# Top-32 attention followed by a SoLU block on one Trainium2 core: the selection of each pair of heads moved one loop step later

## The chip, the cores and the metric

The kernel runs on one core of a Trainium2 chip. The metric is the device time of one execution in microseconds. Before the change it is 2123.96 us, the median of 3 runs (2123.67 to 2125.25). Engines are named as the profile names them: PE (TensorE matmul), PEld (its weight loads), DVE (VectorE), ACT (ScalarE), POOL (GpSimd) and SP (the queue that issues the loads).

## The reference

Attention keeps, in every row of scores, the entries that are not below the 32nd largest; the output goes through a SoLU block.

```python
q, k, v: (8, 8, 576, 64) float32            # batch, heads, seq, head_dim
scores = matmul(q, k.T) / 8
kth    = 32nd largest of each row of scores
scores = where(scores >= kth, scores, -1e9)
attn   = softmax(scores); out = matmul(attn, v)

x  = out as (4608, 512)                      # tokens x (heads * head_dim)
h  = x @ w_in                                # (4608, 1024)
s  = h * softmax(h)
ln = (s - mean(s)) / sqrt(var(s) + 1e-6) * g_ln
y  = ln @ w_out                              # (4608, 512)
```

The weights arrive as 64-bit floats and are converted on the core in the first part of the run.

## The kernel before

Two heads of a batch form a pair; there are 32 pairs (`NPAIR`). A pair has 2 x 576 rows of scores, held as nine row tiles of 128 x 576 (`NT` = 9), in three groups of three (`NG` = 3). The work of a pair i, in functions of the listing:

- `load_qk`, `load_v`: loads of q and k (six transfers) and of v (two), issued on SP.
- `prep`: PE transposes q and k into `qkT`; a few small matmuls give each row a first threshold `t0`, by way of a product `yq`, a DVE sum `ss` and a square root on POOL (`zs`).
- `scores`: PE multiplies into `s_ps`, ACT copies to X (L722), and DVE counts the entries above `t0` (`junkv`, L727). `second` (L735 to L742) makes a better threshold from the counts.
- `count1`: ACT counts against it with a Sign pass that adds up its results (`junka`, L750). `third` (L759 to L767) makes the last threshold `t2`.
- `count2`: ACT's Sign pass against `t2` leaves the signs `sg` (L788) and their sum. Then, in the same function, DVE forms `al` (L793), subtracts it from X and multiplies by the signs (`w`, L799), and takes the eight largest (MAX8, L803): the entries nearest to the threshold, on the side where the 32nd lies.
- `exps`: ACT writes E = exp(X), one instruction for each group (L810). `kth` (from `far`, L816, to L831) picks the 32nd largest from counts and nearest entries.
- `softmax`: DVE masks E by X >= kth and sums it (L841); POOL inverts the sums (`rden`) and scales E (L853).
- `transpose_p`, `transpose_last`, `attn_v`: PE transposes E (`tp_p`, `tp_pt`), ACT copies to PT, and PE multiplies with v (`om`, `ot`); ACT copies the result into `xTm` and `xTt`.

When the four pairs of a batch are done, `queue_batch` appends its token tiles (128 rows of x) to the list `todo`: four tiles, and a fifth with every second batch. A tile has three entries: `mm1` (PE, h_ps, L931), `solu_ln` (DVE, ACT and POOL: hmax, e_sb, solu) and `mm2` (PE `tp_ln` and `o_ps`, L978, then a store). `pop` runs the next entry of the list, if there is one. At first the list holds 18 steps that load and convert the weights.

`slot(i)` joins two pairs: it runs the scores and counts of pair i and the softmax and attention of pair i-1. It is called for i = 0 to 32. Before the change its order is: loads of q and k for pair i+1 and of v for pair i; all scores of i; then for each group `softmax(i-1)`, `count1(i)` alternating with the transposes and attention of i-1, and a pop; then `third(i)`; for each group `count2(i)`, a pop and `exps(i)`; then `prep(i+1)` and `kth(i)`. That is six pops in a full slot.

Nobody writes the engines' queues by hand. The planner of the tile framework walks the program, puts each instruction in its engine's queue when its operands and a buffer for its output are there by the planner's own account, and prefers instructions that stand earlier in the program. On the chip each queue then runs in its order. Buffers are given by tag from a pool: `p1`, `p2`, `p3` and `p6` have 1, 2, 3 and 6 buffers for each tag. X has six (two pairs), E three (one pair), `sg` three (one group), `w` two, q and k two each, `yq` one, s_ps and h_ps share two, in PSUM.

Of the kernel before, what the change touches and what calls it, by code (L numbers as in the profile page):

```python
# [15 lines left out]
P = 128  # L16
# [427 lines left out]
def fast_path(  # L444
# [42 lines left out]
    p2 = ctx.enter_context(tc.tile_pool(name="p2", bufs=2))  # L487
    p3 = ctx.enter_context(tc.tile_pool(name="p3", bufs=3))
    p6 = ctx.enter_context(tc.tile_pool(name="p6", bufs=6))
    small = ctx.enter_context(tc.tile_pool(name="small", bufs=3))  # L490
    ps_big = ctx.enter_context(tc.tile_pool(name="ps_big", bufs=2, space=PS))
    ps_tp = ctx.enter_context(tc.tile_pool(name="ps_tp", bufs=2, space=PS))
# [88 lines left out]
    def load_qk(i):  # L581
        b, hp = pairs[i]
        hh = slice(2 * hp, 2 * hp + 2)
        d = st[i]

        d["q"] = p2.tile([P, NT, D], F32, tag="qm", name="qm")
        d["k"] = p2.tile([P, 2 * NM, D], F32, tag="km", name="km")
        for nm, src in (("q", q), ("k", k)):
            nc.sync.dma_start(
                out=d[nm][:, 0 : 2 * NM, :].rearrange("p (t h) d -> p t h d", h=2),  # L590
                in_=src[b, hh, 0:SM, :].rearrange("h (p t) d -> p t h d", t=NM),
            )
            d[nm + "t"] = p2.tile([ST, 2, D], F32, tag=nm + "t", name=nm + "t")
            nc.sync.dma_start(out=d[nm + "t"], in_=src[b, hh, SM:S, :].rearrange("h p d -> p h d"))
        for h in range(2):
            nc.sync.dma_start(
                out=d["q"][h * ST : (h + 1) * ST, 2 * NM, :], in_=q[b, 2 * hp + h, SM:S, :]
            )
# [10 lines left out]
    def prep(i):  # L609
# [53 lines left out]
                    lhsT=trunc(qkT[hd, 0, qs]), rhs=trunc(mom[hd, :]), start=True, stop=True,  # L663
                )
        ys = [(slice(h, 2 * NM, 2), ys[h]) for h in range(2)] + [(slice(2 * NM, NT), ys[2])]
        yq = p1.tile([P, NT, D], F32, tag="yq", name="yq")
        for js, y in ys:
            nc.vector.tensor_tensor(
                out=yq[:, js, :], in0=y[:, :, 0:D], in1=d["q"][:, js, :], op=ALU.mult
# [25 lines left out]
    def x_of(i, j):  # L695
        return st[i]["X"][j // 3][:, j % 3, :]

    def scores(i, t):

        d = st[i]  # L700
        qkT = d["qkT"]
        tail = t == NM
        if t == 0:
            d["X"] = [None] * NG
            d["c0"] = small.tile([P, NT], F32, tag="c0", name="c0")
        qs = slice(SM, S) if tail else slice(t * P, (t + 1) * P)
        js = [2 * t] if tail else [2 * t, 2 * t + 1]
        big = [ps_big.tile([P, 2, 512], F32, tag="big", name="s_ps") for _ in js]

        for half in range(2):  # L710
            for h in range(2):
                hd = slice(h * D, (h + 1) * D)
                s = big[0][h * ST : (h + 1) * ST] if tail else big[h]
                nc.tensor.matmul(  # L714
                    out=s[:, half, 0:SH], lhsT=qkT[hd, 0, qs],
                    rhs=qkT[hd, 1, half * SH : (half + 1) * SH], start=True, stop=True,
                )
        for j, s in zip(js, big):
            if j % 3 == 0:
                d["X"][j // 3] = p6.tile([P, 3, S], F32, tag="X", name="X")  # L720
            x = x_of(i, j)
            nc.scalar.activation(  # L722
                out=x.rearrange("p (a s) -> p a s", a=2), in_=s[:, :, 0:SH],
                func=AF.Copy, scale=scale,
            )
            junk = p1.tile([P, S], BF16, tag="junkv", name="junkv")
            nc.vector.tensor_scalar(  # L727
                out=junk, in0=x, scalar1=d["t0"][:, j : j + 1], scalar2=None,
                op0=ALU.is_ge, op1=ALU.add, accum_out=d["c0"][:, j : j + 1],
            )  # L730

    def second(i):
        d = st[i]
        r = small.tile([P, NT], F32, tag="r", name="r")
        nc.vector.tensor_scalar(  # L735
            out=r, in0=d["c0"], scalar1=31.5, scalar2=None, op0=ALU.add
        )
        nc.vector.reciprocal(r, r)
        u = small.tile([P, NT], F32, tag="u", name="u")
        nc.vector.tensor_tensor(out=u, in0=r, in1=d["tb"], op=ALU.mult)  # L740
        t1 = small.tile([P, NT], F32, tag="t1", name="t1")
        nc.vector.tensor_tensor(out=t1, in0=u, in1=d["ta"], op=ALU.add)  # L742
        d["u"], d["t1"] = u, t1
        d["n1"] = small.tile([P, NT], F32, tag="n1", name="n1")
        d["n2"] = small.tile([P, NT], F32, tag="n2", name="n2")
# [30 lines left out]
            out=d["tt"], in0=t2, scalar1=2.0, scalar2=1.0, op0=ALU.mult, op1=ALU.mult  # L776
        )

    def count2(i, g):

        d = st[i]
        sg = {}
        for j in range(3 * g, 3 * g + 3):
            sg[j] = p3.tile([P, S], BF16, tag="sg", name="sg")
            nc.scalar.activation(  # L788
                out=sg[j], in_=x_of(i, j), func=AF.Sign, scale=-(1.0 + 2.0**-23),
                bias=d["t2"][:, j : j + 1], accum_out=d["n2"][:, j : j + 1],  # L790
            )
        js = slice(3 * g, 3 * g + 3)
        nc.vector.scalar_tensor_tensor(  # L793
            out=d["al"][:, js], in0=d["n2"][:, js], scalar=512.5, in1=d["tt"][:, js],
            op0=ALU.is_lt, op1=ALU.mult,
        )
        for j in range(3 * g, 3 * g + 3):
            w = p2.tile([P, S], F32, tag="w", name="w")
            nc.vector.scalar_tensor_tensor(  # L799
                out=w, in0=x_of(i, j), scalar=d["al"][:, j : j + 1], in1=sg[j],  # L800
                op0=ALU.subtract, op1=ALU.mult,
            )
            nc.vector.max(d["w8"][:, j, :], w)  # L803
# [206 lines left out]
    def pop():  # L1010
        if todo:
            todo.pop(0)()
# [3 lines left out]
    def slot(i):  # L1016
        new, old = i < NPAIR, i > 0
        if new:
            if i + 1 < NPAIR:
                load_qk(i + 1)  # L1020
            load_v(i)
            for t in range(NM + 1):
                scores(i, t)
            second(i)
        for g in range(NG):
            if old:
                softmax(i - 1, g)
            for j in range(3 * g, 3 * g + 3):
                if new:
                    count1(i, j)  # L1030
                if old:
                    transpose_p(i - 1, j)
                    if j == 3 or j == 7:
                        transpose_last(i - 1, j // 4)
                        attn_v(i - 1, j // 4)
            pop()
        if old:
            transpose_last(i - 1, 2)
            attn_v(i - 1, 2)
        if new:  # L1040
            third(i)
            for g in range(NG):
                count2(i, g)
                pop()
                exps(i, g)
            if i + 1 < NPAIR:
                prep(i + 1)
            kth(i)

    load_qk(0)  # L1050
    prep(0)
# [9 lines left out]


    ok = small.tile([P, 4], F32, tag="ok", name="ok")
    hit = p1.tile([P, NPAIR, NT], F32, tag="yq", name="hit")
    for n, (a, lim, op) in enumerate(
        ((zk_all, 1e-12, ALU.is_gt), (den_all, 1.0, ALU.is_ge), (den_all, 1e30, ALU.is_le))
    ):
# [54 lines left out]
```

## Time and profile before

| | |
|---|---|
| median of 3 runs | 2123.96 us |
| profiled execution, its own time | 2126.24 us |
| its span, first to last instruction | 2124.4 us |
| PE busy | 1522.5 us, 7043 matmuls |
| PEld busy | 847.2 us |
| DVE busy | 1172.9 us, 2816 instructions |
| ACT busy | 1184.7 us, 2398 instructions |
| POOL busy | 649.9 us, 806 instructions |
| mean granted PE clock | 0.795 of full |

The span runs from the first to the last instruction on the core. Busy time is the time in which an engine has an instruction in work. Waits are given as the idle time of the engine just before an instruction, with the instruction whose end let it go on. Line numbers (L799) are those of the listing above. PEclk is the granted TensorE clock as a part of 2.4 GHz; its lower level is 0.5.

### The profile page before, as it was taken

To read this page: it belongs to the slowest core of one execution; us is meant where nothing else is said; L and a number is where in the kernel's file an instruction comes from. 1 tells how busy PE (TensorE), PEld (TensorE's weight loads), DVE (VectorE), ACT (ScalarE), POOL (GpSimd) and SP (SyncE) were. 2 spreads that over 40 slices of the span, in tenths; PEclk is the share of its full clock that TensorE was granted. 3 is DMA by queue.
4 is the path that set the end of the run, shared out by engine and by line. 5 is a ranking of instruction groups with operands and counts; after the bars stand their busy time and mean duration, and the time that the engine had idled before them with its cause. 6 is when DMAs were issued, how large, how long until landed. Compare 5 with 4: busy or idle time off the path is not lost.

```text
span 2124.4 us, 21998 instructions
## 1 busy us (share of the span) xinstructions
PE 1522.5 (72%) x7043; PEld 847.2 (40%) x7043; DVE 1172.9 (55%) x2816; ACT 1184.7 (56%) x2398; POOL 649.9 (31%) x806
## 2 busy tenths in 40 slices
PE   5075558786779777788487785878677877678596
PEld 3043334353334443345243453435333444334343
DVE  4875564565654456555645556456565535655611
ACT  4345555465566455676554565647555755457532
POOL 6776233322312323212233302332232132331221
PEclk8556678976889768896789867988688976889698
DMA  3211000100000100011001010010000100000000
GB/s 103 64 47 38 18 6 17 28 23 18 23 11 18 28 18 23 11 29 28 6 17 28 23 24 6 18 28 23 18 23 11 28 17 18 23 16 11 0 10 17
DMA packets 101900, 48.71 MB, mean 23 GB/s; under 512 B 86920, under 2 KB 95120, under 8 KB 101776
## 3 DMA queue, kind: packets, MB, share of 16 engines
q1 hardware_dynamic: 96528, 37.77, 6.9%
q10 hardware_dynamic: 5248, 9.44, 1.4%
q8 instruction: 59, 0.97, 0.2%
q14 instruction: 65, 0.53, 0.1%
HBM read 37.75 MB, written 9.44 MB: 22 GB/s over the span
## 4 chain that ended last, share of the span: by engine, by line
PE 32%; DVE 27%; ACT 21%; POOL 15%; issue 4%; ACTq 0%; SPq 0%; DMA 0%; DVEq 0%; POOLq 0%
PE o_ps L978 9%; ACT junka L750 8%; DVE w L799 7%; DVE junkv L727 7%; PE om L910 7%; PE s_ps L714 6%; DVE w L803 5%; POOL E L853 4%; ACT sg L788 4%; PE h_ps L931 3%; PE tp_p L870 3%; ACT PT L877 3%; PE tp_ln L972 2%; POOL rden L850 2%; ACT E L810 2%
## 5 line engine op out<-in xcount | busy, mean ns | idle before, releaser
L714 PE MATMUL s_ps<-qkT 64*128 64x288 f32 (+1 forms) x1280 | 367.3, 580 | 34.3 <-ACT X L722 25.6
L870 PE MATMUL tp_p<-ident,E 128*128 128x128 f32 x1152 | 200.7, 315 | 204.9 <-POOL E L853 183.9
L722 ACT ACTIVATE X<-s_ps 128x576 f32<-128x576 f32 x288 | 178.9, 649 | 197.2 <-PE s_ps L714 197.1
L978 PE MATMUL o_ps<-w_out,lnT 128*128 128x512 f32 x576 | 282.8, 648 | 0.0
L750 ACT ACTIVATE junka<-X,t 128x576 bf16<-128x576 f32 x288 | 224.0, 778 | 91.0 <-DVE t L742 88.1
L714 PEld LDWEIGHTS s_ps<-qkT 64*128 64x128 f32 (+1 forms) x1280 | 207.1, 239 | 156.1 <-ACT X L722 98.8
L870 PEld LDWEIGHTS tp_p<-ident,E 128*128 128x128 f32 x1152 | 147.1, 159 | 302.1 <-POOL E L853 212.1
L788 ACT ACTIVATE sg<-X,t 128x576 bf16<-128x576 f32 x288 | 221.9, 773 | 73.3 <-DVE w L799 48.1
L877 ACT COPY PT<-tp_p 128x512 f32<-128x512 f32 x256 | 144.4, 583 | 207.0 <-PE tp_p L870 207.0
L841 DVE SCALAR_TENSOR_TENSOR E<-X,kth,E 128x576 f32<-128x576 f32 x288 | 252.3, 918 | 0.8
L853 POOL TENSOR_SCALAR E<-E,rden 128x576 f32<-128x576 f32 x288 | 247.9, 877 | 9.7
L727 DVE TENSOR_SCALAR_CACHE_REDUCE junkv<-X,t 128x576 bf16<-128x576 f32 x288 | 233.3, 810 | 22.5 <-ACT X L722 6.2
L931 PE MATMUL h_ps<-w_in,xTm 128*128 128x512 f32 x512 | 242.6, 607 | 1.8 <-ACT xTm L916 1.5
L799 DVE SCALAR_TENSOR_TENSOR w<-X,al,sg 128x576 f32<-128x576 f32 x288 | 233.6, 838 | 2.0
L910 PE MATMUL om<-PT,vm 128*64 128x256 f32 x1024 | 188.6, 474 | 62.6 <-ACT PT L877 62.1
L803 DVE MAX8 w<-w 128x8 f32<-128x576 f32 x288 | 208.3, 751 | 1.2
L972 PE MATMUL tp_ln<-ident,solu 128*128 128x128 f32 x288 | 56.7, 351 | 198.4 <-POOL solu L962 197.4
L978 PEld LDWEIGHTS o_ps<-w_out,lnT 128*128 128x128 f32 x576 | 117.8, 210 | 143.1 <-issue 137.9
L810 ACT ACTIVATE E<-X 128x1728 f32<-128x1728 f32 x96 | 157.5, 1640 | 3.6 <-ACT PTt L885 3.3
L775 POOL TENSOR_SCALAR tt<-t 128x9 f32<-128x9 f32 x32 | 6.6, 207 | 479.0 <-DVE t L767 478.8
L957 POOL TENSOR_SCALAR var<-var 128x1 f32<-128x1 f32 x36 | 10.7, 298 | 460.5 <-ACT e_sb L956 460.5
L910 PEld LDWEIGHTS om<-PT,vm 128*64 128x64 f32 x1024 | 94.9, 168 | 135.1 <-ACT PT L877 79.5
(119 smaller groups left out, 1760.9 us busy)
## 6 DMA issues: line engine op xcount, KB each, us to landing
qm<-in_q_dram SPq DMA_DIRECT2D x32, 256.0 KB, 3.4
km<-in_k_dram SPq DMA_DIRECT2D x32, 256.0 KB, 3.4
vm<-in_v_dram SPq DMA_DIRECT2D x32, 256.0 KB, 3.1
out_dram<-osb ACTq DMA_DIRECT2D x32, 256.0 KB, 2.6
w_raw<-in_moe_w_in_dram SPq DMA_DIRECT2D x8, 512.0 KB, 4.0
w_raw<-in_moe_w_out_dram SPq DMA_DIRECT2D x8, 512.0 KB, 3.4
qt<-in_q_dram SPq DMA_DIRECT2D x32, 32.0 KB, 2.3
kt<-in_k_dram SPq DMA_DIRECT2D x32, 32.0 KB, 3.0
```

The costliest lines, as they stand in the source:

```text
L714: nc.tensor.matmul(out=s[:, half, 0:SH], lhsT=qkT[hd, 0, qs], rhs=qkT[hd, 1, half * SH : (half + 1) * SH], start=True, stop=True,)
L727: nc.vector.tensor_scalar(out=junk, in0=x, scalar1=d["t0"][:, j : j + 1], scalar2=None, op0=ALU.is_ge, op1=ALU.add, accum_out=d["c0"][:, j ...
L750: nc.scalar.activation(out=junk, in_=x_of(i, j), func=AF.Sign, scale=-1.0, bias=d["t1"][:, j : j + 1], accum_out=d["n1"][:, j : j + 1],)
L788: nc.scalar.activation(out=sg[j], in_=x_of(i, j), func=AF.Sign, scale=-(1.0 + 2.0**-23), bias=d["t2"][:, j : j + 1], accum_out=d["n2"][:, ...
L799: nc.vector.scalar_tensor_tensor(out=w, in0=x_of(i, j), scalar=d["al"][:, j : j + 1], in1=sg[j], op0=ALU.subtract, op1=ALU.mult,)
L803: nc.vector.max(d["w8"][:, j, :], w)
L841: nc.vector.scalar_tensor_tensor(out=e, in0=x_of(i, j), scalar=d["kth"][:, j : j + 1], in1=e, op0=ALU.is_ge, op1=ALU.mult, accum_out=den_a ...
L853: nc.gpsimd.tensor_scalar(out=e, in0=e, scalar1=d["rden"][:, j : j + 1], scalar2=1.0, op0=ALU.mult, op1=ALU.mult,)
L870: nc.tensor.transpose(tp[:, c, :], pt[:, c * P : (c + 1) * P], ident)
L910: nc.tensor.matmul(out=o[h * D : (h + 1) * D, :], lhsT=vm[:, h, c, :] if c < NM else vt[:, h, :], rhs=rhs[0:ks, c, :], start=(c == 0), sto ...
L931: nc.tensor.matmul(out=h[:, half, :], lhsT=x[:, c, :], rhs=w_in[:, c, half * 512 : (half + 1) * 512], start=(c == 0), stop=(c == NP - 1),)
L978: nc.tensor.matmul(out=o, lhsT=lnT[:, c, :], rhs=w_out[:, c, :], start=(c == 0), stop=(c == NF - 1),)
```

## The change

The functions keep their instructions; their order in `slot` changes, and `count2` is split. `count2(i, j)` is now only the Sign pass of one row tile, whose signs stay in one of nine buffers (`p9`). `nearest(i, g)` holds the DVE part and runs a slot later, with `exps`. The new order of a slot: scores of i, then the loads; then for each group `count1(i)`, `nearest(i-1)`, `exps(i-1)` (in the last group also `third(i)`) and a pop; then `kth(i-1)` and `prep(i+1)`; then for each group `softmax(i-1)`, `count2(i)`, a pop from the second group on, and the transposes and attention of i-1. That is five pops in a full slot. q, k and their tails go from two buffers to one; `yq` and the small tile `hit` at the end share the buffers of `w`.

```diff
+    p9 = ctx.enter_context(tc.tile_pool(name="p9", bufs=9))
...
-        d["q"] = p2.tile([P, NT, D], F32, tag="qm", name="qm")
-        d["k"] = p2.tile([P, 2 * NM, D], F32, tag="km", name="km")
+        d["q"] = p1.tile([P, NT, D], F32, tag="qm", name="qm")
+        d["k"] = p1.tile([P, 2 * NM, D], F32, tag="km", name="km")
...
-            d[nm + "t"] = p2.tile([ST, 2, D], F32, tag=nm + "t", name=nm + "t")
+            d[nm + "t"] = p1.tile([ST, 2, D], F32, tag=nm + "t", name=nm + "t")
...
-        yq = p1.tile([P, NT, D], F32, tag="yq", name="yq")
+        yq = p2.tile([P, NT, D], F32, tag="w", name="yq")
...
-    def count2(i, g):
-        d = st[i]
-        sg = {}
-        for j in range(3 * g, 3 * g + 3):
-            sg[j] = p3.tile([P, S], BF16, tag="sg", name="sg")
-            nc.scalar.activation(
-                out=sg[j], in_=x_of(i, j), func=AF.Sign, scale=-(1.0 + 2.0**-23),
-                bias=d["t2"][:, j : j + 1], accum_out=d["n2"][:, j : j + 1],
-            )
+    def count2(i, j):
+        d = st[i]
+        d["sg", j] = p9.tile([P, S], BF16, tag="sg", name="sg")
+        nc.scalar.activation(
+            out=d["sg", j], in_=x_of(i, j), func=AF.Sign, scale=-(1.0 + 2.0**-23),
+            bias=d["t2"][:, j : j + 1], accum_out=d["n2"][:, j : j + 1],
+        )
+
+    def nearest(i, g):
+        d = st[i]
         js = slice(3 * g, 3 * g + 3)
...
-                out=w, in0=x_of(i, j), scalar=d["al"][:, j : j + 1], in1=sg[j],
+                out=w, in0=x_of(i, j), scalar=d["al"][:, j : j + 1], in1=d.pop(("sg", j)),
...
     def slot(i):
         new, old = i < NPAIR, i > 0
         if new:
+            for t in range(NM + 1):
+                scores(i, t)
             if i + 1 < NPAIR:
                 load_qk(i + 1)
             load_v(i)
-            for t in range(NM + 1):
-                scores(i, t)
             second(i)
+        for g in range(NG):
+            if new:
+                for j in range(3 * g, 3 * g + 3):
+                    count1(i, j)
+            if old:
+                nearest(i - 1, g)
+                exps(i - 1, g)
+            if new and g == NG - 1:
+                third(i)
+            pop()
+        if old:
+            kth(i - 1)
+        if i + 1 < NPAIR:
+            prep(i + 1)
         for g in range(NG):
             if old:
                 softmax(i - 1, g)
             for j in range(3 * g, 3 * g + 3):
                 if new:
-                    count1(i, j)
-                if old:
+                    count2(i, j)
+            if g > 0:
+                pop()
+            if old:
+                for j in range(3 * g, 3 * g + 3):
                     transpose_p(i - 1, j)
                     if j == 3 or j == 7:
                         transpose_last(i - 1, j // 4)
                         attn_v(i - 1, j // 4)
-            pop()
         if old:
             transpose_last(i - 1, 2)
             attn_v(i - 1, 2)
-        if new:
-            third(i)
-            for g in range(NG):
-                count2(i, g)
-                pop()
-                exps(i, g)
-            if i + 1 < NPAIR:
-                prep(i + 1)
-            kth(i)
...
-    hit = p1.tile([P, NPAIR, NT], F32, tag="yq", name="hit")
+    hit = p2.tile([P, NPAIR, NT], F32, tag="w", name="hit")
```

## Rows read from the trace of the kernel before

**Rows 1.** The page, busy us by engine (share of the span) xinstructions.
```profile
PE 1522.5 (72%) x7043; PEld 847.2 (40%) x7043; DVE 1172.9 (55%) x2816; ACT 1184.7 (56%) x2398; POOL 649.9 (31%) x806
```

**Rows 2.** Busy time by stretch (us, each engine's busy us): start, one period, end.
```profile
0.00:452.63 452.63, 269.26 (x1315) 155.92 (x1315) 269.30 (x619) 239.28 (x490) 210.45 (x220) 0.73 0.14 39
...
956.31:1458.06 501.75, 377.29 (x1763) 209.23 (x1762) 282.24 (x687) 295.47 (x599) 134.78 (x179) 0.81 0.08 20
...
1959.82:2124.40 164.58, 119.05 (x451) 62.27 (x450) 56.78 (x140) 58.58 (x111) 35.09 (x49) 0.82 0.03 9
```

**Rows 3.** Busy time by stretch: PE, PEld, DVE, ACT, POOL, then PEclk; slots of a period.
```profile
1010.58:1057.11 46.53, 22.62 (x119) 12.12 (x117) 27.32 (x74) 26.20 (x55) 12.65 (x16) 0.78 0.02 7
1057.11:1122.42 65.31, 55.26 (x235) 29.87 (x237) 36.35 (x89) 37.29 (x76) 18.52 (x25) 0.87 0.06 14
...
1192.21:1270.91 78.70, 59.30 (x284) 35.74 (x284) 41.01 (x100) 44.31 (x90) 19.15 (x25) 0.72 0.13 31
...
sum 501.74, PE 377.28 PEld 209.22 DVE 282.24 ACT 295.47 POOL 134.79; mean PE 47.16 PEld 26.15 DVE 35.28 ACT 36.93 POOL 16.85
```

**Rows 4.** The page's costliest groups: busy us, mean ns of one, idle before.
```profile
L799 DVE SCALAR_TENSOR_TENSOR w<-X,al,sg 128x576 f32<-128x576 f32 x288 | 233.6, 838 | 2.0
L803 DVE MAX8 w<-w 128x8 f32<-128x576 f32 x288 | 208.3, 751 | 1.2
```

**Rows 5.** Waits: who waited for whom, us in total, times, longest us.
```profile
PE tp_ln L972 <- POOL solu L962: 197.4, 20, 12.8
...
DVE al L793 <- ACT sg L788: 215.1, 76, 8.9
DVE step L759 <- ACT junka L750: 209.8, 15, 15.4
```

**Rows 6.** Chain of waits in a light slot, 1010 to 1060: start, us, what.
```profile
1022.89 3.79 POOL E L853 x3
...
1035.50 0.76 ACT junka L750 x2
...
1043.15 1.53 ACT sg L788 x4
...
1045.84 1.55 DVE w L799 x2
```

**Rows 7.** Chain of waits at the end, from 1960 on.
```profile
2012.37 2.32 DVE E L841 x6
...
2022.80 1.11 PE tp_p L870 x4
...
2035.48 0.88 PE ot L910 x20
...
2040.03 1.24 DVE hmax L941
...
2042.91 1.30 DVE solu L949 x2
...
2048.00 1.09 PE tp_ln L972 x8
...
2049.95 6.87 PE o_ps L978 x16
...
2093.48 5.17 PE h_ps L931 x12
```

**Rows 8.** Instructions of PE in order of time: start, us, instruction.
```profile
909.61 1.77 PE L714 MATMUL s_ps<-qkT 64*128 64x288 f32 x8 [0.27 <-ACT X L722]
...
1009.20 2.84 PE L931 MATMUL h_ps<-w_in,xTm 128*128 128x512 f32 x6
```

**Rows 9.** Instructions of DVE in order of time.
```profile
1022.89 0.81 DVE L841 SCALAR_TENSOR_TENSOR E<-X,kth,E 128x576 f32<-128x576 f32 x1
...
1024.77 1.29 DVE L841 SCALAR_TENSOR_TENSOR E<-X,kth,E 128x576 f32<-128x576 f32 x1
```

**Rows 10.** The page's DMA issues: transfer, queue, count, KB each, us to landing.
```profile
qm<-in_q_dram SPq DMA_DIRECT2D x32, 256.0 KB, 3.4
```

## The prediction

> **What bounds the kernel now.** I read the page's busy line first: PE is the busiest engine at 72% [rows 1], and no engine is full. An average over different stages says little, so I next took busy times by stretch. After a start of 453 us the kernel repeats itself every eight pairs, in 501.75 us; three such periods run, and 164.6 us are left at the end [rows 2]. One period is then cut at the first instruction of each `kth`, which gives slots of 46.5 to 78.7 us [rows 3]. Their lengths go with the token work: a slot with next to none takes 46.5 us and PE is busy for 22.6 of it. A slot with about two token tiles takes 65.3 us with PE busy 55.3 (85%), and the longest, 78.7 us, has PE at 59.3 (75%) and a clock of 0.72.
>
> So there are two kinds of slot. The light one is a chain, which the critical path shows step by step: the POOL scaling of E, then `count1`'s Sign passes on ACT taking turns with the PT copies, then the Signs of `count2`, and only then DVE's w [rows 6]. DVE is idle from about 1026 to 1045.8 us there [rows 6, 9], because its next work, `nearest` of the same pair, needs both counts. The waits name it: DVE's `step` waited 209.8 us for the Signs of `count1`, `al` waited 215.1 us for those of `count2` [rows 5]. Over 32 pairs that is 13.3 us a pair. The heavy slot is set mostly by PE, in part by PE waiting behind a token tile's normalisation: 197.4 us of `tp_ln` on POOL's `solu` [rows 5].
>
> One thing about order has to be known before a moved line is priced. The engines' queues are not in program order. At 1009.2 us PE runs six h_ps matmuls of a token tile, the three chunks whose x exists [rows 8]; the pair that completes the fourth has not had its E scaled by then (1022.9 us [rows 6]). So the planner pulls later work forward when its operands and buffers are there, and program order acts as a priority.
>
> **The change, part by part.**
>
> *Selection one slot later (slot's new order).* Per pair the same instructions run on every engine; what goes is dependence. In the first half of slot i, ACT does `count1(i)` while DVE does `nearest(i-1)`, 9 x (838 + 751) ns = 14.3 us [rows 4], whose signs were made in the slot before. In the second half DVE does `softmax(i-1)` while ACT does `count2(i)`. Both DVE waits, 13.3 us a pair, should go. Check on a light slot: 46.5 - 13.3 = 33.2 us. DVE's own work gives the same: 282.24 / 8 = 35.3 us a slot [rows 3], less 9/8 of a token tile's two large passes and small ones (1.24 + 1.30 + about 0.5) [rows 7], is 31.9. With the contention below, 33.3. What is late next is DVE itself or ACT (295.47 / 8 = 36.9 with tokens [rows 3]), each with some waiting for scores and for `third`. I take 38 us for a light slot; ends 33.3 (no wait left) and 46.5 (no gain).
>
> *Pops, five in place of six per slot.* A tile is three pops. On PE at full clock it costs 16 h_ps matmuls, 16/12 x 5.17 = 6.9 us, 8 transposes 1.1 and 16 o_ps 6.9: 14.9 us [rows 7]. A batch queues 12 pops, every second one 15, which now come as 5, 5, 2, 0 and 5, 5, 5, 0: five heavy slots, one middling and two light ones per period. A heavy slot has a third of a tile less than the 65.3 us one: PE 55.3 - 5.0 = 50.3 us of work. If PE keeps that slot's 85%, it takes 59.4, say 60 us. Ends: 50.3 (PE never waits) and 67 (the 75% of the longest slot). I stay at 85%, the best that any slot shows: the PE gaps that DVE caused will shrink, but three pops in a row (matmul, normalisation, matmul) again put PE behind an 8.0 us chain, from hmax at 2040.0 to `tp_ln` at 2048.0 [rows 7]. The middling slot has 10 us of PE more than a light one, which fits under DVE: 43 us.
>
> *All nine signs kept.* `count2`'s Sign instructions no longer wait for DVE to free one of three buffers; they run ahead of the PT copies on ACT. No instruction is added. It is what allows the overlap and is priced in it.
>
> *DVE beside POOL.* `nearest` can now run beside the E scaling of the pair before. A softmax pass takes 0.81 us alone and 1.29 beside POOL [rows 9], so 0.48 us each. Bounds: 0 to 9 x 0.48 = 4.3 us a slot; I take three passes, 1.4 us, since only POOL's last group can meet the next selection, and it counts only where DVE sets the end. The Trainium skill (SBUF — State Buffer, "Who interferes with whom") says that a DVE instruction with two SBUF inputs contends with a GpSimd one that reads SBUF, and that the loser blocks fully for the other's whole instruction. By that rule each of the nine w passes could wait out a POOL scaling, 3.79 / 3 = 1.26 us beside DVE work [rows 6]: 11.4 us a slot, 10 more than taken, and over nine slots that DVE sets a total near 1937 us. The rows agree that the two delay each other, but the delay is 0.48 us, not a whole instruction.
>
> *q and k in single buffers, loads behind `scores`.* `load_qk(i+1)`, six DMAs on SP, now waits until `prep(i)` has read its tiles; on SP `load_v(i)`, two DMAs, stands behind it, wanted only by `attn_v(i)` a slot later. A big transfer lands 3.4 us after issue [rows 10]. `prep(i)` ends about a slot before `prep(i+1)` starts, so I cost this at 0. With that cover gone, if prep is pulled far forward, it is one landing, 3.4 us a slot. A gain is excluded, since the loads only start later than before.
>
> *yq (and hit) in w's buffers.* For four short DVE instructions a pair only one w buffer is left. Between 0 and about 1 us a slot (w and MAX8 then take turns singly); 0 taken, since DVE has other work to put between.
>
> *Start and end.* The 18 weight steps take four slots in place of three, and POOL is busy 210 us in the first 453 [rows 2]; no gain there. Three of the seven first slots gain like the rest. At the end slot 32 now does `nearest(31)` and the exponentials before its softmax, but slot 31 no longer does. The chain from `scores(31)` to the last attention is as long as before: 0, give or take 15 us.
>
> **Sum**, against the profiled execution's own 2126.2 us (span 2124.4, some 2 us around it). A period becomes 5 x 60 + 43 + 2 x 38 = 419 us in place of 501.75: 82.8 less, three times 248. The start gives 3 x 82.8 / 8 = 31. 2126.2 - 248 - 31 = 1847; the median of the runs stands 2 us lower: 1845 us.
>
> **Rivals.**
>
> *A: PE keeps most of it.* Transposes, attention, prep, the next scores and two pops all stand in the second half, and PE's queue runs in its order: a token matmul that waits for `solu` holds up what follows. For it: the 75% slot and the 197 us on `tp_ln`. Against: before, the token pieces stood in both halves too. Then heavy slots take 67 us, the middling 52, light ones 44: 475 a period, 27 less, and some 10 at the start: about 2035 us (1980 to 2110).
>
> *B: slower: the halves stay one behind the other.* Place: the border in the middle of a slot, where `softmax(i-1)` needs `kth(i-1)`, and that all of `nearest(i-1)`. If PE has no scores to run while it waits for E, a heavy slot is: first half matmul 6.9, normalisation 8.0, transposes and matmul with a piece of the next tile 8.9, together 23.8; second half from the first softmax pass to the first transposes 10.4, to the end of attention 13.6 [rows 7], scores between 8.9 (five times 1.77 [rows 8]) and half as much again, say 11, and two pops 14.9: 49.9. That is 73.7 us. A light slot is 14.3 + 35 = 49.3, the middling 52. A period then takes 519 us, 17 more; with the start about 2190 us. It decides from 2.2 us of overlap per slot downwards. For it: the selection of a pair really is one block now. Against: the planner's early matmuls [rows 8], six X buffers that let `scores(i+1)` start as `softmax(i-1)` frees them, and nine signs that let `nearest` follow at once.
>
> *C: nothing happens.* If the planner's order is set by operands alone, queues come out alike: 2124 us. The three sign buffers speak against it, as they forbade the new order.
>
> *D: PE dense.* The heavy slots at 53 us, light at 34: 1715 us.
>
> **How the numbers follow.** Forecast 0.60, its own range 1735 to 1980 (heavy slots 55 to 65, light ones 35 to 43); A 0.16, B 0.17, C 0.03, D 0.04. The range 1735 to 2110 holds the forecast and A. Faster by over 0.2% (what a measurement here can tell from no change): 0.60 + 0.16 + 0.04 = 0.80; within 0.2% 0.03; slower 0.17.
>
> **What would show it.** In the trace after: `step` and `al` waiting less than 60 us each in place of 210; DVE's w of one pair beside the Signs of `junka` of the next; light slots near 38 us and heavy ones near 60; PE's share of the span above 80% (72% now), since its work stays and the span shrinks; no wait on DMA for q or k. It is wrong if DVE still idles over 10 us a slot between two softmax groups and `nearest`, if PE's waits for E or for `solu` grow, or if light slots stay at 46 us.

## The result, and the profile after

The changed kernel takes 1764.69 us, the median of 4 runs (1762.15 to 1767.68), against 2124.61 us for the kernel before in the same runs. The ratio is 0.8306, with a 95% interval of 0.8289 to 0.8323: 360 us less. The forecast was 1845 us, 80 us too much.

The page's busy line of the kernel after answers to [rows 1].

```profile
PE 1423.9 (81%) x7043; PEld 782.8 (44%) x7043; DVE 1155.7 (65%) x2816; ACT 1175.2 (67%) x2398; POOL 647.3 (37%) x806
```

The instructions are the same in number on each engine. PE's busy time fell by 98.6 us all the same: the granted clock is higher (see the stretches below), and most of the same matmuls take less time.

To see where the 360 us came from, both spans are cut at the same two instructions, the first of `kth(7)` and of `kth(31)` (`far`): start, 24 pairs, end. The columns are those of [rows 2]: the stretch and its length, busy us of PE, PEld, DVE, ACT and POOL with their instructions, the granted clock, and two figures of the DMA (its busy share and GB/s). First the kernel after.

```profile
0.00:421.62 421.62, 274.45 (x1444) 156.63 (x1445) 293.18 (x701) 265.31 (x550) 228.85 (x242) 0.79 0.16 43
421.62:1645.77 1224.15, 1056.50 (x5267) 580.67 (x5267) 832.41 (x2047) 877.12 (x1793) 396.54 (x534) 0.89 0.09 24
1645.77:1764.70 118.93, 92.95 (x338) 45.48 (x334) 30.11 (x72) 32.74 (x57) 21.86 (x30) 0.90 0.04 12
```

And the same cut in the kernel before.

```profile
0.00:508.64 508.64, 316.88 (x1529) 184.41 (x1530) 302.48 (x703) 276.89 (x566) 225.83 (x242) 0.72 0.14 38
508.64:2006.43 1497.79, 1118.53 (x5220) 619.83 (x5218) 840.95 (x2048) 880.30 (x1783) 402.21 (x534) 0.82 0.07 19
2006.43:2124.40 117.97, 87.07 (x295) 42.92 (x295) 29.49 (x70) 27.46 (x49) 21.91 (x30) 0.86 0.04 12
```

The start saved 87.0 us, the 24 pairs 273.6 and the end lost 1.0. A period of eight pairs in the kernel after is the third line here; the first two are its shortest and its longest slot. They answer to [rows 3].

```profile
876.60:909.21 32.61, 26.26 (x94) 13.11 (x93) 20.85 (x56) 22.89 (x51) 14.19 (x19) 0.87 0.04 10
...
973.70:1040.22 66.52, 61.30 (x293) 33.25 (x292) 45.62 (x107) 45.67 (x89) 18.83 (x25) 0.90 0.09 23
...
884.33:1293.92 409.59, 352.70 (x1762) 194.23 (x1761) 278.86 (x687) 292.76 (x599) 133.04 (x179) 0.88 0.09 25
```

A period went from 501.75 to 409.59 us. Its slots, from `far` to `far`, are 45.4, 32.6, 64.5, 66.5, 46.7, 35.6, 62.7 and 55.6 us. In the longest PE is busy 92% of the time: there little but PE's own work is left.

The waits of DVE in the kernel after answer to [rows 5] (who waited for whom, us in total, times, longest us).

```profile
DVE step L760 <- ACT junka L751: 134.2, 20, 9.2
DVE al L795 <- ACT sg L783: 91.1, 32, 7.0
DVE junkv L728 <- ACT X L723: 78.0, 46, 5.3
...
DVE yq L669 <- PE tp_y L662: 33.9, 13, 3.3
```

The third, DVE's count behind the copy to X, was 6.2 us before. PE's largest waits are three of 50 to 63 us, and one that is new, `tp_p` behind DVE's t (L681), 27 times.

```profile
PE tp_ln L974 <- POOL solu L964: 63.0, 17, 8.1
PE tp_p L872 <- POOL E L855: 59.7, 7, 24.5
PE s_ps L715 <- ACT X L723: 50.0, 50, 17.3
PE tp_p L872 <- DVE t L681: 47.2, 27, 3.7
```

The kernel before had three times as much in the second of these.

```profile
PE tp_p L870 <- POOL E L853: 183.9, 22, 54.7
```

**What runs beside what.** Next DVE's instructions in the kernel after (start, us, instruction, idle before it in brackets).

```profile
899.72 0.16 DVE L795 SCALAR_TENSOR_TENSOR al<-n,tt 128x3 f32<-128x3 f32 x1 [2.57 <-POOL tt L776]
906.85 0.16 DVE L795 SCALAR_TENSOR_TENSOR al<-n,tt 128x3 f32<-128x3 f32 x1 [6.97 <-ACT sg L783]
...
914.91 0.42 DVE L669 TENSOR_TENSOR yq<-tp_y,qm 128x256 f32<-128x256 f32 x1 [2.83 <-PE tp_y L662]
...
915.72 0.81 DVE L801 SCALAR_TENSOR_TENSOR w<-X,al,sg 128x576 f32<-128x576 f32 x1
...
922.37 0.76 DVE L805 MAX8 w<-w 128x8 f32<-128x576 f32 x1
923.04 0.80 DVE L728 TENSOR_SCALAR_CACHE_REDUCE junkv<-X,t 128x576 bf16<-128x576 f32 x1
...
940.43 0.82 DVE L843 SCALAR_TENSOR_TENSOR E<-X,kth,E 128x576 f32<-128x576 f32 x1
...
941.17 0.81 DVE L728 TENSOR_SCALAR_CACHE_REDUCE junkv<-X,t 128x576 bf16<-128x576 f32 x1
```

ACT in the same stretch: the first and the last Signs of `count2(17)`, X of pair 18, then `count1(18)`.

```profile
896.07 0.77 ACT L783 ACTIVATE sg<-X,t 128x576 bf16<-128x576 f32 x1
...
908.24 0.76 ACT L783 ACTIVATE sg<-X,t 128x576 bf16<-128x576 f32 x1
...
915.76 1.19 ACT L723 ACTIVATE X<-s_ps 128x576 f32<-128x576 f32 x2 [0.51 <-PE s_ps L715]
...
949.53 0.78 ACT L751 ACTIVATE junka<-X,t 128x576 bf16<-128x576 f32 x1 [5.59 <-DVE t L743]
```

In the kernel before, a pair ends on DVE before the next one has begun.

```profile
1137.06 0.81 DVE L841 SCALAR_TENSOR_TENSOR E<-X,kth,E 128x576 f32<-128x576 f32 x1
...
1148.10 0.42 DVE L668 TENSOR_TENSOR yq<-tp_y,qm 128x256 f32<-128x256 f32 x1 [10.22 <-PE tp_y L661]
```

So the overlap that came is not the one that was planned. `nearest(17)` stands a slot after `count2(17)` in the program, but the planner pulled it forward: its first `al` is there 3.65 us after the first Sign of `count2(17)` (896.07), and all of it is done (939.39) before `count1(18)` begins (949.53). What lies beside it is the next pair's prep and scores: w, MAX8 and the masked E of pair 17 alternate with `junkv` of pair 18, while before DVE finished pair 17, stood still for 10.2 us, and only then got yq of pair 18. Worked out from the start and length of each instruction over one period, w and MAX8 beside `junka` are 0.0 us before and 0.0 after; masked E beside `junka` went from 0.3 to 13.0 us, PT copies beside w and MAX8 from 3.4 to 23.8. The time in which just one of PE, DVE and ACT was busy fell from 149.5 to 36.0 us per period, that with all three rose from 102.7 to 161.1.

### The profile page after: what moved, and what is told of

It reads as the page before. It is cut to its first block, busy times and chain, and to the rows that moved or that the text cites. A ratio compares the mean times of both kernels' runs of the same rounds, so it can differ in the third digit from the quotient of the medians.

```text
span 1764.7 us, 21722 instructions
## 1 busy us (share of the span) xinstructions
PE 1423.9 (81%) x7043; PEld 782.8 (44%) x7043; DVE 1155.7 (65%) x2816; ACT 1175.2 (67%) x2398; POOL 647.3 (37%) x806
## 4 chain that ended last, share of the span: by engine, by line
PE 38%; DVE 22%; ACT 16%; POOL 15%; issue 7%; DMA 1%; SPq 0%; ACTq 0%; DVEq 0%; POOLq 0%
PE o_ps L980 9%; PE om L912 8%; PE tp_p L872 8%; PE s_ps L715 7%; ACT junka L751 7%; DVE junkv L728 5%; DVE E L843 5%; POOL zs L678 3%; ACT sg L783 3%; DVE w L801 3%; POOL E L855 3%; DVE w L805 2%; POOL solu L964 2%; PE tp_pt L890 2%; PE tp_ln L974 2%
## 5 line engine op out<-in xcount | busy, mean ns | idle before, releaser
L715 PE MATMUL s_ps<-qkT 64*128 64x288 f32 (+1 forms) x1280 | 335.8, 483 | 70.6 <-ACT X L723 50.0
L872 PE MATMUL tp_p<-ident,E 128*128 128x128 f32 x1152 | 206.6, 330 | 117.9 <-POOL E L855 59.7
L980 PE MATMUL o_ps<-w_out,lnT 128*128 128x512 f32 x576 | 264.9, 612 | 0.0
L872 PEld LDWEIGHTS tp_p<-ident,E 128*128 128x128 f32 x1152 | 156.7, 168 | 209.3 <-issue 96.2
L933 PE MATMUL h_ps<-w_in,xTm 128*128 128x512 f32 x512 | 232.1, 597 | 0.6 <-ACT xTm L918 0.6
L715 PEld LDWEIGHTS s_ps<-qkT 64*128 64x128 f32 (+1 forms) x1280 | 161.1, 195 | 157.9 <-ACT X L723 80.7
L849 POOL TENSOR_SCALAR rden<-den_all 128x3 f32<-128x3 f32 x96 | 30.9, 322 | 542.0 <-DVE E L843 467.6
L723 ACT ACTIVATE X<-s_ps 128x576 f32<-128x576 f32 x288 | 178.4, 650 | 68.9 <-PE s_ps L715 56.6
L805 DVE MAX8 w<-w 128x8 f32<-128x576 f32 x288 | 209.8, 750 | 0.0
L980 PEld LDWEIGHTS o_ps<-w_out,lnT 128*128 128x128 f32 x576 | 110.4, 197 | 133.7 <-issue 126.3
L812 ACT ACTIVATE E<-X 128x1728 f32<-128x1728 f32 x96 | 157.6, 1647 | 12.2 <-PE tp_pt L890 12.1
L912 PE MATMUL om<-PT,vm 128*64 128x256 f32 x1024 | 161.7, 454 | 0.1
L933 PEld LDWEIGHTS h_ps<-w_in,xTm 128*128 128x128 f32 x512 | 93.2, 190 | 103.8 <-issue 98.7
L912 PEld LDWEIGHTS om<-PT,vm 128*64 128x64 f32 x1024 | 89.3, 165 | 59.2 <-issue 39.0
```

The lines of the kernel that those rows point to most:

```text
L715: nc.tensor.matmul(out=s[:, half, 0:SH], lhsT=qkT[hd, 0, qs], rhs=qkT[hd, 1, half * SH : (half + 1) * SH], start=True, stop=True,)
L872: nc.tensor.transpose(tp[:, c, :], pt[:, c * P : (c + 1) * P], ident)
L912: nc.tensor.matmul(out=o[h * D : (h + 1) * D, :], lhsT=vm[:, h, c, :] if c < NM else vt[:, h, :], rhs=rhs[0:ks, c, :], start=(c == 0), sto ...
L933: nc.tensor.matmul(out=h[:, half, :], lhsT=x[:, c, :], rhs=w_in[:, c, half * 512 : (half + 1) * 512], start=(c == 0), stop=(c == NP - 1),)
L980: nc.tensor.matmul(out=o, lhsT=lnT[:, c, :], rhs=w_out[:, c, :], start=(c == 0), stop=(c == NF - 1),)
```

## The experiments

The theory of the first runs: the new order makes the gain, with `prep(i+1)` ahead of the transposes of pair i-1 as what lets the next scores start early, and with the kept signs. Rivals: the buffers alone; the order alone; the selection's place alone. The spread of the token work is a question beside it.

**Buffers alone, in the old order (`b_sg9`).** The kernel before with nine sign buffers, single q and k, and yq in w's buffers.

```diff
+    p9 = ctx.enter_context(tc.tile_pool(name="p9", bufs=9))
-            sg[j] = p3.tile([P, S], BF16, tag="sg", name="sg")
+            sg[j] = p9.tile([P, S], BF16, tag="sg", name="sg")
...
```

> The kernel before with all buffer changes and none of the new order: nine sign buffers, q and k single, yq in w's buffers. Theory (the order does it: count1 of one pair beside the selection of the pair before): 2090 to 2130 us; the 48 us that ACT's sg waited for DVE's w go, but step and al wait about as long as before (210 and 215 us). Rival (the planner ignores program order where it can, so the sign buffers alone free it): 1765 to 1850 us, with step and al waiting under 140 and 95 us.

2127.39 us against 2123.85, ratio 1.0015 [1.0005, 1.0025]: no gain. The order is needed. One part of the expectation failed: `al` waited 141.9 us in place of 215, and nothing was won by it, since `yq` (176.6 us, 136.1 before) and others waited longer.

**The new order with three sign buffers (`a_sg3`).**

```diff
-        d["sg", j] = p9.tile([P, S], BF16, tag="sg", name="sg")
+        d["sg", j] = p3.tile([P, S], BF16, tag="sg", name="sg")
```

> The changed kernel with three sign buffers in place of nine. Theory (order and kept signs are needed together): the Signs of groups 1 and 2 must wait for DVE's w of the same pair a slot later, so DVE's waits in al come back; 1900 to 2060 us. Rival (the order alone brings it, the signs of one group are enough of a lead): 1765 to 1800 us.

1811.62 us, 0.8524 [0.8510, 0.8539]. The theory was wrong and the rival near (12 us above its range): only 47 of the 360 us hang on the kept signs. ACT waits for DVE to free a sign buffer, a wait that the kernel after does not have.

```profile
ACT sg L783 <- DVE w L801: 34.4, 27, 7.4
```

**The new order with prep at the slot's end (`a_prep_end`).**

```diff
-        if i + 1 < NPAIR:
-            prep(i + 1)
         for g in range(NG):
...
             attn_v(i - 1, 2)
+        if i + 1 < NPAIR:
+            prep(i + 1)
```

> The changed kernel with prep(i+1) moved from the middle of the slot to its end, behind the attention of pair i-1. Theory (the two halves overlap because the next scores run on PE in the second half; prep's early place allows it): scores come late, 4 to 10 us a slot more, 1890 to 2080 us. Rival (place is only a priority and PE has gaps, so the planner pulls prep forward all the same): 1755 to 1800 us.

2070.15 us, 0.9745 [0.9729, 0.9761]. One moved call gives back 305 of the 360 us, as expected. DVE now stands before yq, and PE before the transposes.

```profile
DVE yq L669 <- PE tp_y L662: 395.9, 28, 20.4
...
PE tp_p L872 <- POOL E L855: 372.1, 50, 44.7
```

PE's order shows what may hold prep back: its first transpose (`tp_t`) comes only behind the last transpose of pair i-1 (`tp_pt`), in all 30 cases, by 1.7 to 2.2 us in the repeated part.

```profile
1160.12 0.27 PE L886 MATMUL tp_pt<-ident,E 128*64 128x128 f32 x1
...
1161.97 0.27 PE L618 MATMUL tp_t<-ident,qt 64*128 64x64 f32 x1
```

DVE's order shows a second hold. `al` of pair 17 is there at 1076.86, but its first w comes only behind yq of pair 18, with DVE idle before.

```profile
1076.86 0.25 DVE L795 SCALAR_TENSOR_TENSOR al<-n,tt 128x3 f32<-128x3 f32 x2 [4.76 <-POOL tt L776]
...
1098.22 0.42 DVE L669 TENSOR_TENSOR yq<-tp_y,qm 128x256 f32<-128x256 f32 x1 [11.17 <-PE tp_y L662]
...
1099.02 0.81 DVE L801 SCALAR_TENSOR_TENSOR w<-X,al,sg 128x576 f32<-128x576 f32 x1
```

Over 31 pairs these delays from the first `al` to the first w add up to 720.9 us, and in 30 of them w starts within 1.5 us of yq; in the kernel after they are 107.3 us, before 1.8. So in `a_prep_end` the selection of pair i stands behind `prep(i+1)`, and that behind the attention of pair i-1. That yq now takes its buffer from w's would explain it (see the next section); no run of the new order gave yq a buffer of its own.

**The same with prep's PSUM tiles in the scores' buffers (`a_prep_end_big`).** `tp_t`, `tp_qk`, `tp_m` and `tp_y` leave the two buffers that they share with the transposes; the small y_t moves into `tp_y`'s tile.

```diff
-        tails = ps_tp.tile([P, NM, P], F32, tag="tp", name="tp_t")
+        tails = ps_big.tile([P, NM, P], F32, tag="big", name="tp_t")
...
```

> The changed kernel with prep(i+1) at the end of the slot, as in the run that took 2070 us, but with its PSUM tiles in the buffers of the scores in place of those of the transposes. Theory (the place decided because the two PSUM buffers of the transposes are handed out in program order, so prep could not start before the last transposes of the slot): most of the 305 us comes back, 1765 to 1900 us, with prep's transposes ahead of the last tp_pt of a slot. Rival (the place decides as a priority on PE): 2030 to 2100 us.

1903.99 us, 0.8969 [0.8954, 0.8984], 4 us above the expected range: 166 of the 305 us come back, with prep still last in the program. Its transposes now run ahead, in all 30 cases.

```profile
1043.03 0.27 PE L618 MATMUL tp_t<-ident,qt 64*128 64x64 f32 x1
...
1060.26 0.27 PE L886 MATMUL tp_pt<-ident,E 128*64 128x128 f32 x1
```

So moving prep out of the two `tp` buffers is worth a good half of what its place cost. The other 139 us stay open: w is still held up behind yq (398.4 us over 31 pairs), and here prep shares buffers with the scores, which has a price of its own (`s_ps` waits 52.8 us for DVE's t).

**The old order with prep moved forward (`b_prep_mid`).**

```diff
             second(i)
+            if i + 1 < NPAIR:
+                prep(i + 1)
...
-            if i + 1 < NPAIR:
-                prep(i + 1)
             kth(i)
```

> The kernel before with one part of the new order alone: prep(i+1) stands behind second(i), ahead of softmax and transposes; selection stays in its slot. Theory (two things are needed, scores that can run early and a selection that waits for neither count of its own pair): 2000 to 2110 us, with step and al still waiting over 150 us each. Rival (prep's place is the whole of it): 1765 to 1900 us.

1963.00 us against 2123.57, 0.9244 [0.9228, 0.9259]: 161 us, between the two expectations; `al` waited 197.0 us, `step` 127.1 and not over 150. With the selection a slot later and prep at the end (`a_prep_end`) it is 54 us. Both together are 360, so 145 us come only from the two jointly, if prep's place ahead of `softmax` is taken as the same in both orders. The largest wait of PE in this kernel is a new one: the scores that prep lets loose stand on PE and wait for the copy to X, up to 34.1 us at a time (25.6 us in total before).

```profile
PE s_ps L714 <- ACT X L722: 189.7, 121, 34.1
```

**Token entries spread evenly (`a_even`).** Three or four pops in every slot in place of five while there are any.

```diff
+    quota = [0]
     def pop():
-        if todo:
+        if todo and quota[0] > 0:
+            quota[0] -= 1
             todo.pop(0)()
...
+        quota[0] = 5 if i <= NP else -(-len(todo) // (NP - (i - NP - 1) % NP))
...
```

> The changed kernel with the token entries of a batch spread evenly over the four slots up to the next batch: 3 a slot, or 4, 4, 4 and 3, in place of 5, 5, 2, 0 and 5, 5, 5, 0. Theory (heavy slots are set by PE, light ones by DVE and ACT, so evening out uses the PE that idles in light slots): a period of eight pairs 380 to 395 us in place of 409.6, 1680 to 1725 us in all. Rival (each token tile costs its fixed time wherever it stands): 1755 to 1785 us.

1900.27 us, 0.8951 [0.8935, 0.8966]: 136 us slower than the kernel after, and both expectations wrong. Slots came out more even, but not evenly (44.8 to 66.9 us in a period, five of the eight between 55 and 60), and with the three pops of a slot in its first half, a tile's `mm2` stood right behind its own normalisation.

```profile
PE tp_ln L974 <- POOL solu L964: 215.1, 27, 14.4
```

**The same, at most two pops in the first half (`a_even2`).**

```diff
-            pop()
+            if i <= NP or g < 2:
+                pop()
```

> The evenly spread token entries as in the run that took 1900 us, but two of them at most in the first half of a slot and the others in the second, so that a tile's normalisation runs beside prep and softmax. Theory (the 1900 us came from PE standing behind each tile's normalisation, 215 us of waits in tp_ln against 63): tp_ln waits under 90 us and 1680 to 1765 us. Rival (spreading itself costs, since scores of the next pair find one of two PSUM buffers taken by h): 1850 us and more.

1755.48 us, 0.8266 [0.8252, 0.8279], as expected: 145 us less than `a_even`, and a little better than the kernel after. So the place of the pops made `a_even` slow, not the spread.

```profile
PE tp_ln L974 <- POOL solu L964: 13.0, 4, 8.1
```

**Each tile's `mm2` queued behind the next tile's `mm1` (`a_skew`).**

```diff
+    late = []
...
         todo.append(lambda: mm1(d, x))
+        todo.extend(late)
         todo.append(lambda: solu_ln(d))
-        todo.append(lambda: mm2(d, stores))
+        late[:] = [lambda: mm2(d, stores)]
...
```

> The changed kernel with five pops as it is, but each tile's last entry (mm2) put behind the next tile's mm1, so that PE has a matmul to run during a normalisation. Theory (PE's waits for solu, 63 us, and what hangs on them go): 1715 to 1755 us. Rival (the planner pulls the next tile's mm1 forward already, and a second h tile takes the scores' PSUM): 1765 to 1830 us.

1727.52 us (1726.97 to 1729.18), 0.8137 [0.8124, 0.8151]: 37 us less than the kernel after, and the best kernel here. The 63.0 us of waits that it aimed at are gone; `step`'s fell too, from 134.2 to 54.0, and so did the delay of w behind yq, from 107.3 to 38.3, so the 37 us are not those of `tp_ln` alone.

```profile
PE tp_ln L974 <- POOL solu L964: 0.8, 1, 0.8
```

**That with prep right behind `second` (`a_skew_prep`).** The idea was to start prep still earlier.

```diff
             second(i)
+            if i + 1 < NPAIR:
+                prep(i + 1)
...
-        if i + 1 < NPAIR:
-            prep(i + 1)
```

> The version that took 1727.5 us (each tile's mm2 behind the next tile's mm1) with prep(i+1) placed still earlier, right behind second(i). Theory (the earlier the next pair's prep, the earlier its scores, and ACT's count1 still waits 115 us for second): 1680 to 1715 us. Rival (the scores cannot start before softmax frees X, so nothing is won, and prep's DVE work now delays the selection): 1725 to 1770 us.

1977.99 us, 0.9313 [0.9297, 0.9328]: 250 us slower than `a_skew`, and both expectations wrong. The transposes wait for E seven times as long as in `a_skew` (59.2 us), and DVE waits for X in small pieces.

```profile
PE tp_p L872 <- POOL E L855: 422.8, 57, 51.1
...
DVE junkv L728 <- ACT X L723: 397.3, 164, 11.7
```

Of the three places tried in the new order, the middle is the best, and earlier is not better. Which resource turns it is not isolated.

**Weight conversion left out (`b_noconv`, `a_noconv`).** In both kernels one DVE copy of the upper words takes the place of the conversion of the 64-bit weights, so the weights are not the right ones, and POOL (about 105 us over the run) and DVE (about 35) have less to do at the start.

```diff
-            tmp = p2.tile([P, 2, 512], F32, tag="solu", name="w_tmp")
-            mi = p1.tile([P, DFF], F32, tag="e", name="w_mi")
-            yield from float64_stages(
...
+            yield
+            nc.vector.tensor_copy(out=dst, in_=w_raw.pop(n).bitcast(F32)[:, 1::2])
```

> The kernel before without the conversion of the weights from 64-bit floats (one DVE copy of the upper words stands in its place; the loads stay, the weights are meaningless). It tells what set the first slots. Theory (the pair's own chain set them, and the conversion ran beside it on POOL): 2100 to 2125 us. Rival (POOL's conversion set them, as the prediction assumed): 2020 to 2075 us.

2061.15 us against 2124.04, 0.9708 [0.9689, 0.9727]: the conversion costs the kernel before 63 us. The rival's range was right; that POOL's part of the conversion sets the slots, and not DVE's, is not shown by it.

> The changed kernel without the conversion of the weights (a DVE copy of the upper words in its place). Theory (with the pair's chain shortened, the conversion now sets the first slots): 1690 to 1730 us, so that more is saved here than in the kernel before. Rival (hidden in both): 1750 to 1765 us.

1714.83 us, 0.8077 [0.8061, 0.8093]: it costs the kernel after 50 us, inside the expected range, but less than in the kernel before, where more was expected. So of the 87 us that the start saved, some 13 are a better hidden conversion; the other 74 come from the first slots themselves. The kernel after leads by 2.2 us at `kth(0)`, and in the seven slots from there to `kth(7)` it gains -0.1, 20.4, 19.9, 3.1, 32.4, 3.6 and 5.6 us.

**Attention alone (`a_notok`).** The changed kernel without any token tile; the output is not written.

```diff
-            if hp == NP - 1:
-                queue_batch(b)
```

> The changed kernel without any token tile (attention alone, weights still loaded; the output is not written). Theory (a slot without token work is set by DVE's own 32 to 33 us and some waits): slots of 33 to 37 us, 1130 to 1250 us in all. Rival (with PE idle more its clock falls, and transposes and scores at the lower clock make the chain longer): slots of 38 us and more, over 1280 us.

1396.86 us, 0.6579 [0.6565, 0.6594], slots of 39.3 to 40.9 us each in the repeated part. Four of them, from `far` to `far`:

```profile
913.42:1075.54 162.12, 117.38 (x702) 72.69 (x700) 124.31 (x318) 125.63 (x268) 53.97 (x76) 0.75 0.10 24
```

The rival's time was right: a slot without tokens takes 40.5 us, though no engine is busy for over 78% of it, so waits between engines still set it. The clock is lower, as the rival said (0.75), but how much of the slot that makes is not separated. The light slots of the kernel after (34.1 us on average) are shorter than this: a part of their pairs' work runs in the heavy slots beside them. The 36 token tiles add 368 us, 10.2 us each, though a tile has 14.9 us of matmuls at full clock [rows 7]: by this estimate about a third of the token work fits into the gaps of attention.

## Why the prediction was right or wrong

*That the gain comes from DVE's waits for the counts: right in sign, wrong in mechanism.* The step that failed is "in the first half of slot i, ACT does `count1(i)` while DVE does `nearest(i-1)`". The planner pulled `nearest(i-1)` to where its operands were, and the two never met: 0.0 us in a period. Where they do meet, the kernel is not a fast one: worked out in the same way over the whole run, w and MAX8 lie beside `junka` for 75.4 us in `a_prep_end` and 114.4 in `a_skew_prep`, which take 2070 and 1978 us, and for 7.1 in the kernel after. The prediction had named that pulling itself, from the early h_ps matmuls [rows 8], and did not apply it to the line that was moved. What the place of `nearest` in the program did change is the priority. `prep(i+1)` and what follows from it now stand ahead of the transposes and masked products of i-1, and the runs show that this place of prep is the condition: without it 54 us are left, with it alone 161. By how much it acts through the `tp` buffers, through w's, and as a priority is open beyond the 166 us of `a_prep_end_big`.

*Waits under 60 us each: missed.* `step` went from 209.8 to 134.2 us and `al` from 215.1 to 91.1 (and 12.9 more behind POOL's `tt`), some 187 us together, in place of 305 or more. The rest came from waits that the prediction did not count: `yq` for prep's products (136 before, 33.9 after), `tp_p` for E (183.9 to 59.7), `tp_ln` for `solu` (197.4 to 63.0), and, on ACT, X for the scores (197.1 to 56.6). DVE's wait for X grew from 6.2 to 78.0. PE's waits for E and `solu` fell and PE's share of the span came to 81%, as the prediction asked, and no single wait of DVE in the period is over 8.9 us (15.4 before). Waits on different engines overlap and can't be added.

*The period: 409.6 us against 419, near, by other parts.* The terms were five slots of 60, one of 43 and two of 38. There are four long ones (62.3 on average), two middling (46) and two light (34.1). The pops do not fix where a token piece runs, since PE takes its matmuls early; that errors cancel here is luck in part. "Keeps that slot's 85%" was mis-sized: a heavy slot has PE busy 88 to 92% of the time, with the scores of the next pair to fill it.

*PE's clock was in no term.* PE's 377.3 us in a period became 352.7 with the same matmuls, at a granted clock of 0.88 in place of 0.81. This bears directly on the slots that PE sets.

*The start: 31 us predicted, 87 measured.* This is 56 of the 80 us by which the forecast was off; the 24 pairs are another 26. The mis-sized step is "Three of the seven first slots gain like the rest". The seven gained 12.1 us each on average, a slot of the period 11.5, though very unevenly; and some 13 us of the conversion, whose slots the prediction took as bound by POOL, are better hidden.

*The end: 0 predicted, 1.0 us longer.* Right.

*Signs: "what allows the overlap"; mis-sized.* They are worth 47 us.

*q and k in single buffers: 0, right.* No load of either appears among the waits beyond the first pair's (4.6 and 0.9 us, once each), and in the old order all buffer edits together cost 0.15%.

*DVE beside POOL: less than taken.* Over a period no w pass lies beside a POOL scaling of E, before or after. w and the masked E are on average no longer than before (838 ns for w in [rows 4]); first E before, then both after:

```profile
L841 DVE SCALAR_TENSOR_TENSOR E<-X,kth,E 128x576 f32<-128x576 f32 x288 | 252.3, 918 | 0.8
...
L843 DVE SCALAR_TENSOR_TENSOR E<-X,kth,E 128x576 f32<-128x576 f32 x288 | 250.5, 898 | 15.9 <-ACT E L812 13.3
...
L801 DVE SCALAR_TENSOR_TENSOR w<-X,al,sg 128x576 f32<-128x576 f32 x288 | 229.5, 823 | 0.6
```

The 1.4 us a light slot did not come: planned neighbours did not become neighbours. Nor was it right to set 0.48 us of delay against a whole scaling of 1.26: in the trace of the kernel before the 181 scalings of E without any DVE work beside them take 0.75 us on average, and those beside a masked E 1.15, so the 1.26 us already hold a wait of POOL for DVE. The Trainium skill (SBUF — State Buffer, "Who interferes with whom") states that a DVE instruction with two SBUF inputs contends with a GpSimd instruction that reads SBUF, and calls the shared ports an exclusive lock; these lengths agree. It had no pair of w and E scaling to act on over a period, and no run here shows what it would cost there.

*yq in w's buffers: 0 to 1 us a slot was likely too little.* In the kernel after, the first w of a pair never starts before yq of the next pair's prep, in 31 of 31 cases. In the rows above `al` was there at 899.72 and w came at 915.72, right behind yq at 914.91, with DVE idle for 6.97 and 2.83 us between. The delays from first `al` to first w add up to 107.3 us over the 31 pairs; in `b_sg9`, which shares the buffers too but has this work ahead of prep in the program, to 1.3 us, and in `a_prep_end`, with prep later, to 720.9. That buffers are given in program order would explain it, but the new order with a buffer for yq alone was not tried: the delay is measured, its cause argued, and how much of it costs time is open. The prediction looked here for w and MAX8 taking turns, and not for a selection that waits for the next pair's prep.

*The new wait.* `tp_p` behind DVE's t, 47.2 us: prep, now ahead of the transposes, holds both `tp` buffers until POOL's square root (1.8 us) and t0 are done. The prediction had looked at DVE and SP for what the moved prep holds up, and not at the PSUM buffers.

*Rivals.* A, PE keeps most of it, needed heavy slots of 67 us and light ones of 44; B needed the halves to stay one behind the other, and the border that it prices, `softmax` after all of `nearest`, is crossed by the next pair's `junkv`. C and D lie 360 us and 50 us away. D's light slots (34) came, its heavy ones (53) did not.

## What to carry to other kernels

Where a planner takes what is ready, moving a line changes its priority and its claim on shared buffers, and its time only through these: before pricing an overlap, ask what will be ready first, and which buffers the moved block takes ahead of its neighbours. Look for the block that everything later waits for (here the next pair's transposes and thresholds), and try its place by itself in both orders; of three places here the middle one was the best. A chain of matmul, normalisation and matmul wants another tile's matmul between its ends: putting it there was worth 37 us here, and a spread that set the three right behind one another cost 136.

## What was not expected of the hardware

The same 576 matmuls of `o_ps`, each 128x512, took 648 ns on average in the kernel before:

```profile
L978 PE MATMUL o_ps<-w_out,lnT 128*128 128x512 f32 x576 | 282.8, 648 | 0.0
```

In the kernel after they took 612 (busy us, mean ns, idle before):

```profile
L980 PE MATMUL o_ps<-w_out,lnT 128*128 128x512 f32 x576 | 264.9, 612 | 0.0
```

Over a period PE was busy 24.6 us less with the same work, at a granted clock of 0.88 in place of 0.81, while its busy share of the period rose from 75% to 86%. In attention alone, with PE busy 72% of four slots, the clock was 0.75. How full PE is does not settle the clock, though: over the whole span it was 0.851 in `a_prep_end` with PE busy 70%, and 0.799 in `b_prep_mid` with 79%. So part of what the removed waits gave came back in this form, 24.6 of the period's 92.2 us at the most, and which change of order raises the clock is open.
